# Constant key rows written as 32-bit words and shared by two engines, the plane join on GpSimd, one low part in six on ScalarE, and a new instruction order

## The chip, the cores and the metric

The kernel runs on one core of a Trainium2 chip. The metric is the device time of one execution in microseconds (us). The engines are TensorE (PE in the rows, its weight loads PEld), VectorE (DVE), ScalarE (ACT), GpSimd (POOL) and SyncE (SP), which issues every DMA of this kernel.

## The reference

Eight batches of eight attention heads (1152 keys of 64 values, queries averaged in pairs to 576 rows), then a channel mix over the joined heads.

```
q_pool = q.reshape(B, H, S // 2, 2, D).mean(axis=3)
scores = (q_pool @ k^T) / sqrt(D);  scores -= max(scores)
attn = exp(scores) / (sum(exp(scores)) + 1e-09);  a = attn @ v
x = a joined over heads            # 8 x 576 x 512
xk = mu_k * x + (1 - mu_k) * x_prev;  xr = mu_r * x + (1 - mu_r) * x_prev
out = sigmoid(xr @ w_r) * (relu(xk @ w_k) ** 2 @ w_v)
```

All inputs are fp32. The weights are 512x1024, 1024x512 and 512x512.

## The kernel before

The 64 heads run one after another. Each head has six blocks of 96 query rows, and a block has nine key chunks of 128. Operands are split into a high and a low half in fp16, so that products keep nearly fp32 accuracy.

**One block.** TensorE multiplies the keys (`ks1`) by the queries into a score buffer `s` in PSUM, of which there are three (L602). VectorE takes the maximum over the keys: in the first 14 heads (`n < N_ROW`) with L612, two small matmuls and a ScalarE instruction (L615 to L622), after that with L627 and four short steps that end at L648. The maximum goes into rows of the second query operand, and a second pass of matmuls with `ks2` (L653) adds the low halves and takes the maximum away. ScalarE writes the exponentials `pf` (L660). GpSimd writes their low part `pl` (L663) from the low 16 bits. TensorE multiplies both by the values (L741, L743 and L748 for whole windows of 128 rows, L712 for the half windows), in one PSUM bank `a`.

**The key buffers.** `ks2` has two buffers, for even and odd heads. Partitions 64 to 127 come by DMA from `ks1` (L551). Partitions 0 to 63 hold constants that never change: zeros, with one value in partition 0 and another in partition 1. They are written once, ahead of everything else, by three memsets on VectorE for each buffer (L448 to L450).

**Joining heads.** Two heads make a group `g` of four. For groups 4 to 30 of 32 (`CROSS`), `crossed` splits the fp32 result into two 16-bit planes (`xp`, L791), transposes them by DMA into `xd`, and joins the planes again into `xt` with three copies (L802): two of 64x128 elements and one of 128x1024. All of that runs on ScalarE before. The other five groups are turned by TensorE (L818).

**The channel mix.** When a batch of heads is finished, its rows go through two mixes (L953 to L964) and three products (L985), in tiles of 256 rows. This matmul work is spread between the blocks of the heads that follow. At the start the weights, which come as 64-bit floats, are decoded to fp16 pairs by ScalarE, VectorE and GpSimd (L856 to L874).

**The order.** Every operation is recorded by `op(engine, duration, function, ...)` with the buffers that it reads and writes. `Issue.run` then plays the list with the stated durations and chooses the order in which each engine issues its instructions. `MOVES`, `SEED` and `SPREAD` change priorities in that play at pseudo-random, each entry of `MOVES` in one stretch of time; three quarters of the entries fall within the first 170 us of the plan. The order is fixed in the program: an engine whose next instruction waits issues nothing behind it. What stands ahead of the recorded operations (constants, memsets) is issued first, in program order, on each engine.

Of the kernel before, what the change touches and what calls it, by code (L numbers as in the profile page):

```python
# [4 lines left out]

# [16 lines left out]
P = 128  # L22
# [17 lines left out]
CROSS = range(4, 31)  # L40
N_ROW = 14
PAIR = 99
GA = 0.045
XM = 3
SPLIT_ENG = 'ACT'
JOIN_ENG = 'ACT'
HALF_ENG = "ACT"
CROSS_LOAD, CROSS_MORE = 2.1, 0.5

# [38 lines left out]
WDEP = [("ks1", 1), ("ks2", 0), ("vr", 1)]  # L88
AHEAD2 = 0
MOVES, BASE, REACH = (  # L90
    34, 51, 119, 147, 174, 176, 191, 263, 328, 478, 600, 742, 785, 805, 941, 956, 1439, 1609, 3150, 4342,
    5377, 6334, 7410, 9224, 10224, 10571, 13731, 15873, 16751, 17268, 19136, 22188, 24107, 24376, 25583,
    25931, 31593,
), 2000000, 1150.0
SEED, SPREAD = 7, 1.0


class Issue:
# [224 lines left out]
def kernel(  # L323
# [63 lines left out]
    for a in range(P // U):  # L387
        part = slice(a * U, (a + 1) * U)
        nc.vector.memset(mask[part, a + 1:a + 2], 1.0 / SM)
        nc.gpsimd.tensor_copy(gather[part], ident[part, part].unsqueeze(1).broadcast_to([U, P // U, U]))  # L390
    nc.vector.memset(mask[0:U, 0:1], 1.0 / SM)

    kr, vr = bufs("kr", 2, [P, NC, D], F32), bufs("vr", 2, [P, NC, D], F32)
# [48 lines left out]
        nc.gpsimd.memset(t_[:, 1, :, 0:D], 0.0)  # L442
    for t_ in mx:
        nc.vector.memset(t_[:, 0:P - QN], 0.0)
    for t_ in md:
        nc.gpsimd.memset(t_, 0.0)
    for t_ in ks2:
        nc.vector.memset(t_[0:D], 0.0)  # L448
        nc.vector.memset(t_[0:2], -SM * 2.0 * EPS)
        nc.vector.memset(t_[0:1], -SM * (1.0 - EPS))  # L450
    for t_ in vt:
        nc.vector.memset(t_[:, :, 2 * D:2 * D + 2], 1.0)
    for t_ in vb:
# [128 lines left out]
    def block(n, j, i, t):  # L582

        hp, z = n % 2, i % 3
        qi = n // 2 % 2
        q0 = hp * TQ + j * QN
        qhi, qlo = (qT[qi][:, r].rearrange("p j x -> p (j x)")[:, q0:q0 + QN] for r in (0, 1))
        kh, kl = ([(t_, qi, c) for c in range(q0 // P, (q0 + QN - 1) // P + 1)] for t_ in ("qT", "qTl"))
        qm = [("qm", qi, q0)]
        s = s_b[z]  # L590
        p0 = (0 if hp else HW) + j * QN
        rows, us = slice(p0, p0 + QN), range(p0 // U, (p0 + QN) // U)

        def cols(c0, c1):
            return s[:, P + c0 * QN:P + c1 * QN]

        def grid(c0, c1):
            return cols(c0, c1).rearrange("p (c q) -> p c q", q=QN)

        def scores(c0, c1):  # L600
            for c in range(c0, c1):
                nc.tensor.matmul(cols(c, c + 1), ks1[hp][:, c, :], qhi,  # L602
                                 start=(c == c0), stop=False, skip_group_check=True)

        def first():
            for c0, c1 in BK:
                op("PE", (c1 - c0) * 0.0430, lambda c0=c0, c1=c1: scores(c0, c1),
                   r=[("ks1", hp), ("ks1", hp, 5)] + kh, w=[("s", z)], key=t)

        def row():  # L610
            mxz, mbz, y = mx[i % 2], mb[z], i % 2
            op("DVE", 0.975, lambda: nc.vector.tensor_reduce(mxz[:, P - QN:P], grid(0, NC).rearrange("p c q -> p q c"),  # L612
                                                             axis=AX.X, op=ALU.max),
               r=[("s", z)], w=[("mx", y)], key=t)
            op("PE", 0.059, lambda: nc.tensor.matmul(s[:, 0:P], mxz, identb, start=False, stop=False, skip_group_check=True),  # L615
               r=[("mx", y)], w=[("s", z)], key=t + O_MAX)
            op("DVE", 0.199, lambda: nc.vector.tensor_reduce(mbz, s[:, 0:P], axis=AX.X, op=ALU.max),
               r=[("s", z)], w=[("mb", z)], key=t + O_MAX)
            op("PE", 0.047, lambda: nc.tensor.matmul(s[:, 0:QN], mbz.broadcast_to([P, P]), negi[:, P - QN:P],
                                                     start=False, stop=False, skip_group_check=True),  # L620
               r=[("mb", z)], w=[("s", z)], key=t + O_MAX)
            op("ACT", 0.153, lambda: nc.scalar.activation(qlo[0:1], s[0:1, 0:QN], getattr(AF, ROW),  # L622
                                                          scale=(1.0 + EPS) / (1.0 - EPS), alpha=(1.0 - EPS) / (1.0 + EPS)),
               r=[("s", z)] + kl, w=qm, key=t + O_MAX)

        def top(y, a):
            op("DVE", 0.972, lambda: nc.vector.tensor_reduce(  # L627
                my[y][:, a], cols(0, NC).rearrange("p (x q) -> p x q", q=U), axis=AX.X, op=ALU.max, apply_transpose=True),
               r=[("s", z)], w=[("my", y)], key=t)

        def join(y, m):
            ql = qT[qi][0:U, 1].rearrange("p j x -> p (j x)")[:, q0 + QN - m * QN:q0 + QN]
            kls = kl if m == 1 else [("qTl", qi, c) for c in range((q0 - QN) // P, (q0 + QN - 1) // P + 1)]
            qms = [("qm", qi, q0 - x * QN) for x in range(m)]
            mr, got = s[:, 0:3 * m], s[0:U, U:U + 18 * m].rearrange("p (j k) -> p j k", k=6)
            mqz = mq[y][:, 0:3 * m]
            op("DVE", 0.062 + 0.028 * m, lambda: nc.vector.tensor_reduce(
                mr.rearrange("p (a j) -> p a j", j=3), my[y][:, 0:m].rearrange("p a (c j) -> p a j c", j=3), axis=AX.X, op=ALU.max),
               r=[("my", y)], w=[("s", z)], key=t + O_MAX)
            op("DVE", 0.061 + 0.019 * m, lambda: nc.vector.tensor_tensor(  # L640
                mqz, mr.unsqueeze(2).broadcast_to([P, 3 * m, 6]), mask.unsqueeze(1).broadcast_to([P, 3 * m, 6]), op=ALU.mult),
               r=[("s", z)], w=[("mq", y)], key=t + O_MAX)
            op("PE", GA, lambda: nc.tensor.matmul(s[:, U:U + 18 * m], gather.rearrange("p a x -> p (a x)"),
                                                  mqz.rearrange("p j k -> p (j k)"), start=False, stop=False, skip_group_check=True),
               r=[("mq", y)], w=[("s", z)], key=t + O_MAX)
            op("DVE", 0.055 + 0.031 * m, lambda: nc.vector.tensor_reduce(
                md[y][:, 0:3 * m, 0:2], windows(got, 5), axis=AX.X, op=ALU.max), r=[("s", z)], w=[("md", y)], key=t + O_MAX)
            op("DVE", 0.072 + 0.1 * m, lambda: nc.vector.transpose(ql, md[y][:, 0:3 * m].rearrange("p j x -> p (j x)")),  # L648
               r=[("md", y)] + kls, w=qms, key=t + O_MAX)

        def scores2(c0, c1):
            for c in range(c0, c1):
                nc.tensor.matmul(cols(c, c + 1), ks2[hp][:, c, :], qlo,  # L653
                                 start=False, stop=True, skip_group_check=True)

        def second():
            for c0, c1 in BK:
                op("PE", (c1 - c0) * 0.0430, lambda c0=c0, c1=c1: scores2(c0, c1),
                   r=[("ks2", hp)] + kl + qm, w=[("s", z)], key=t + O_EXP)
            op("ACT", NC * QN / 1200 + 0.06, lambda: nc.scalar.activation(  # L660
                pf[:, :, rows], grid(0, NC), AF.Exp, bias=SHIFT, scale=0.125 / (2.0 * SQ)),
               r=[("s", z)], w=[("pf", x) for x in us] + [("gate", i)], key=t + O_EXP)
            op("POOL", NC * QN / 1000 + 0.12, lambda: nc.gpsimd.tensor_scalar(  # L663
                pl[:, :, rows], half(pf, U16, 0)[:, :, rows], LO, 1.0, op0=ALU.mult, op1=ALU.mult),
               r=[("pf", x) for x in us], w=[("pl", x) for x in us], key=t + O_REST, port=True)

        return first, row, top, join, second

# [59 lines left out]
    def window(n, w, t):  # L728
# [37 lines left out]
        op("DVE", 0.08, lambda: nc.vector.reciprocal(dz, dz), r=[("den", z)], w=[("den", z)], key=t + O_EVAC)  # L766
        if n < X_ACT:
            for k_ in range(nk):
                op("ACT", 0.051 + D / 1200, lambda k_=k_: nc.scalar.activation(
                    xb[0][:, 2 * (k0 + k_) + hh], u[:, k_, 0:D], AF.Copy, scale=dz[:, k_:k_ + 1]),  # L770
                   r=[("den", z), ka], w=[("xb", 2 * (k0 + k_) + hh)], key=t + O_EVAC)
        else:
            op("DVE", 0.07 + nk * D / 960, lambda: nc.vector.tensor_tensor(  # L773
                xb[0][:, 2 * k0 + hh:2 * NW:2], u[:, :, 0:D], dz.unsqueeze(2).broadcast_to([P, nk, D]), op=ALU.mult),
               r=[("den", z), ka], w=[("xb", 2 * k_ + hh) for k_ in range(k0, NW)], key=t + O_EVAC)
# [2 lines left out]

    def copier(e, n):

        return {"POOL": (0.12 + n * 0.00113, nc.gpsimd.tensor_copy), "ACT": (0.093 + n / 1200, nc.scalar.copy),
                "DVE": (0.07 + n / 960, nc.vector.tensor_copy)}[e]

    def crossed(b, g, t):
# [268 lines left out]
        return key  # L1053


    queries(0, -20.0)
    prep(0, -20.0)
    prep(1, -10.0)
# [76 lines left out]
```

## Time and profile before

| | |
|---|---|
| median of 3 runs | 1095.19 us (1095.1 to 1096.24) |
| the profiled execution: its time | 1096.61 us |
| the profiled execution: its span | 1094.8 us |
| mean granted clock of TensorE | 0.995 |
| busy: PE, DVE, ACT, POOL | 1052.2, 920.7, 878.2, 593.6 us |
| read from HBM, written | 67.11 MB, 9.44 MB |

The span runs from the first to the last instruction, and 1.81 us of the execution's time lie outside it. Busy time of TensorE counts an instruction from its start to its modelled end, with overlaps counted once, so a high share does not say that its array is full. The granted clock is 1.0 for 2.4 GHz and 0.5 for 1.2 GHz; a value between them is a mean over a stretch.

### The profile page before, as it was taken

The page shows a single profiled execution, that of the slowest core. Times are in us where ns is not written, and L with a number is a line of the kernel's source. Part 1 is how long each engine was busy: PE and PEld are TensorE (multiplying, and loading weights), DVE is VectorE, ACT ScalarE, POOL GpSimd, SP SyncE. Part 2 cuts the span into 40 slices and gives each one's busy share as a digit, 9 for nine tenths or more (in the row PEclk, how much of TensorE's full clock was granted, in tenths as well). Part 3 has the DMA queues.
Part 4 walks back from the last instruction along what each step waited for, and adds up shares of the span by engine and source line. Part 5 has one row for each costly group of instructions (what it writes and reads, how often), then busy time and mean ns, then how long its engine had stood idle before and what let it go on. Part 6 is the DMA issues. An engine that isn't in the chain of part 4 may idle for free.

```text
span 1094.8 us, 43933 instructions
## 1 busy us (share of the span) xinstructions
PE 1052.2 (96%) x18521; PEld 858.5 (78%) x18521; DVE 920.7 (84%) x2400; ACT 878.2 (80%) x1604; POOL 593.6 (54%) x641
## 2 busy tenths in 40 slices
PE   5888899999999999999999999999999999999998
PEld 4777887978688887888787888878787978787565
DVE  8889888989899989998998998998889899975321
ACT  6999998978778888888887788887788887865643
POOL 3556685645555464654565465656465645554431
PEclk9999999999999999999999999999999999999999
DMA  8998955666666538674675655565656654510000
GB/s 204 234 233 201 192 131 130 140 142 111 134 124 121 123 71 179 128 132 79 143 157 100 143 125 124 122 141 113 134 113 130 143 116 89 90 40 12 20 28 22
DMA packets 254166, 134.52 MB, mean 123 GB/s; under 512 B 189456, under 2 KB 226320, under 8 KB 253968
## 3 DMA queue, kind: packets, MB, share of 16 engines
q1 hardware_dynamic: 253968, 131.71, 57.6%
q8 instruction: 145, 2.38, 0.9%
q14 instruction: 53, 0.43, 0.1%
HBM read 67.11 MB, written 9.44 MB: 70 GB/s over the span
## 4 chain that ended last, share of the span: by engine, by line
PE 82%; ACT 5%; DVE 5%; DMA 2%; issue 2%; POOL 0%; ACTq 0%; DVEq 0%
PE f L985 34%; PE s L602 11%; PE s L653 11%; PE a L748 5%; PE a L743 5%; PE a L741 5%; PE s L985 5%; ACT pf L660 2%; PE a L712 2%; PE a L985 2%; DMA ks<-kn 2%; DVE my L627 1%; ACT xt L802 1%; DVE mx L612 1%; DVE xm L956 1%
## 5 line engine op out<-in xcount | busy, mean ns | idle before, releaser
L663 POOL TENSOR_SCALAR pl<-pf 128x864 f16<-128x864 uint16 x384 | 384.3, 1001 | 360.0 <-ACT pf L660 322.4
L660 ACT ACTIVATE pf<-s 128x864 int32<-128x864 f32 x384 | 335.1, 887 | 89.2 <-PE s L653 40.2
L627 DVE TRANSPOSE_TENSOR_REDUCE my<-s 128x27 f32<-128x864 f32 x300 | 319.9, 1072 | 48.7 <-PE s L602 35.9
L602 PE MATMUL s<-qT,ks 128*128 128x96 f16 x3456 | 216.7, 207 | 11.7 <-ACT pf L660 10.6
L653 PE MATMUL s<-qT,ks 128*128 128x96 f16 x3456 | 211.5, 207 | 3.8 <-ACT qT L622 2.9
L602 PEld LDWEIGHTS <-ks 128*128 128x128 f16 x3456 | 181.5, 98 | 41.4 <-issue 16.0
L653 PEld LDWEIGHTS <-ks 128*128 128x128 f16 x3456 | 177.6, 98 | 26.8 <-issue 5.1
L743 PE MATMUL a<-vt,pf 128*128 128x64 f16 x2304 | 192.0, 194 | 0.4 <-issue 0.4
L741 PE MATMUL a<-vt,pf 128*128 128x65 f16 x2304 | 191.5, 193 | 0.4 <-DVE xb L773 0.4
L741 PEld LDWEIGHTS <-pf 128*128 128x128 f16 x2304 | 160.1, 99 | 4.6 <-issue 0.7
L743 PEld LDWEIGHTS <-pf 128*128 128x128 f16 x2304 | 154.7, 98 | 6.4 <-issue 1.2
L985 PE MATMUL f<-xhk,wk_hi 128*128 128x256 f16 x496 | 135.0, 272 | 0.0
L985 PE MATMUL f<-xlk,wk_hi 128*128 128x256 f16 x496 | 135.0, 272 | 0.0
L985 PE MATMUL f<-xhk,wk_lo 128*128 128x256 f16 x496 | 135.0, 272 | 0.0
L748 PE MATMUL a<-vb,pl 128*128 128x65 f16 x2304 | 122.8, 193 | 0.1
L985 PEld LDWEIGHTS <-wk_hi 128*128 128x128 f16 x1152 | 105.0, 98 | 11.5 <-issue 0.5
L1016 POOL TENSOR_TENSOR gl<-g 128x512 f16<-128x512 f32 x72 | 78.9, 1097 | 55.5 <-ACT g L1014 53.6
L748 PEld LDWEIGHTS <-pl 128*128 128x128 f16 x2304 | 97.3, 98 | 6.0 <-POOL pl L663 0.3
L612 DVE TENSOR_REDUCE mx<-s 128x96 f16<-128x864 f32 x84 | 87.3, 1052 | 16.3 <-PE s L602 5.6
L985 PE MATMUL f<-wv_hi,g 128*128 128x512 f16 x240 | 90.8, 378 | 2.1 <-ACT ex L1033 2.0
L985 PE MATMUL f<-wv_lo,g 128*128 128x512 f16 x240 | 90.9, 379 | 0.0
L985 PE MATMUL f<-wv_hi,gl 128*128 128x512 f16 x240 | 90.9, 379 | 0.0
(130 smaller groups left out, 2095.1 us busy)
## 6 DMA issues: line engine op xcount, KB each, us to landing
kr<-in_k_dram SPq DMA_DIRECT2D x64, 288.0 KB
vr<-in_v_dram SPq DMA_DIRECT2D x64, 288.0 KB
qr<-in_q_dram SPq DMA_DIRECT2D x63, 256.0 KB
ks<-ks SPq DMA_DIRECT2D x64, 144.0 KB
out_dram<-em SPq DMA_DIRECT2D x36, 256.0 KB
xt<-in_moe_w_k_dram SPq DMA_DIRECT2D x8, 512.0 KB
xt<-in_moe_w_v_dram SPq DMA_DIRECT2D x8, 512.0 KB
qr<-in_q_dram SPq DMA_DIRECT2D x32, 64.0 KB
```

Source lines behind the costliest of these rows:

```text
L602: nc.tensor.matmul(cols(c, c + 1), ks1[hp][:, c, :], qhi, start=(c == c0), stop=False, skip_group_check=True)
L612: op("DVE", 0.975, lambda: nc.vector.tensor_reduce(mxz[:, P - QN:P], grid(0, NC).rearrange("p c q -> p q c"), axis=AX.X, op=ALU.max), r=[( ...
L627: op("DVE", 0.972, lambda: nc.vector.tensor_reduce(my[y][:, a], cols(0, NC).rearrange("p (x q) -> p x q", q=U), axis=AX.X, op=ALU.max, app ...
L653: nc.tensor.matmul(cols(c, c + 1), ks2[hp][:, c, :], qlo, start=False, stop=True, skip_group_check=True)
L660: op("ACT", NC * QN / 1200 + 0.06, lambda: nc.scalar.activation(pf[:, :, rows], grid(0, NC), AF.Exp, bias=SHIFT, scale=0.125 / (2.0 * SQ)) ...
L663: op("POOL", NC * QN / 1000 + 0.12, lambda: nc.gpsimd.tensor_scalar(pl[:, :, rows], half(pf, U16, 0)[:, :, rows], LO, 1.0, op0=ALU.mult, o ...
L712: nc.tensor.matmul(a_b[z * HW:(z + 1) * HW, x0:x1], tb[:, c, p0:p0 + HW], vs[(n - 1 + z) % NV][:, c, r0:r0 + x1 - x0], skip_group_check=Tr ...
L741: nc.tensor.matmul(bank[:, a0:a0 + VN], half(pf, F16, 1)[:, c, rows], vt[jv][:, c, D:D + VN], start=(w == 1 and c == 0 and hh == 0), stop= ...
L743: nc.tensor.matmul(bank[:, a0:a0 + D], half(pf, F16, 1)[:, c, rows], vt[jv][:, c, 0:D], start=False, stop=False, skip_group_check=True)
L748: nc.tensor.matmul(bank[:, a0:a0 + VN], pl[:, c, rows], vb[jv][:, c, 0:VN], start=False, stop=(c == NC - 1), skip_group_check=True)
L985: nc.tensor.matmul(ps, terms[i][0], terms[i][1], start=(first and i == 0), stop=(i == last), skip_group_check=True)
L1016: op("POOL", 2 * n * 0.00203 + 0.08, lambda f2=f2: nc.gpsimd.tensor_tensor(gl[:, f2, 0:n], g32[:, f2, 0:n], gh[:, f2, 0:n], op=ALU.subtrac ...
```

## The change

1. The constant rows are written by a function `rows(engine, tile)`: zeros as before, and the two constant values as pairs of fp16 packed into one 32-bit word, so that a row is 576 words and not 1152 values. VectorE writes the first buffer ahead of everything. GpSimd writes the second, as a recorded operation.
2. The casts that fill `gather` and the memsets of `md` leave the prologue and become one recorded operation on GpSimd.
3. `JOIN_ENG` is `POOL`: the 128x1024 plane copy of L802 goes to GpSimd. The two 64x128 copies stay on ScalarE.
4. `PL_J = (5,)`: from head 14 on, the low part `pl` of the last of a head's six blocks is written by ScalarE.
5. The stated durations of some operations are altered, and `MOVES`, `SEED` with them, so the whole order is new.

```diff
-GA = 0.045
+GA = 0.03
+PL_J = (5,)
...
-JOIN_ENG = 'ACT'
+JOIN_ENG = 'POOL'
...
-    34, 51, 119, 147, 174, 176, 191, 263, 328, 478, 600, 742, 785, 805, 941, 956, 1439, 1609, 3150, 4342,
...
+    34, 54, 55, 67, 78, 129, 145, 371, 393, 692, 792, 1668, 1700, 2452, 3169, 3236, 3417, 3712, 4201, 4456,
...
-SEED, SPREAD = 7, 1.0
+SEED, SPREAD = 41, 1.0
...
-        nc.gpsimd.tensor_copy(gather[part], ident[part, part].unsqueeze(1).broadcast_to([U, P // U, U]))
...
-    for t_ in md:
-        nc.gpsimd.memset(t_, 0.0)
-    for t_ in ks2:
-        nc.vector.memset(t_[0:D], 0.0)
-        nc.vector.memset(t_[0:2], -SM * 2.0 * EPS)
-        nc.vector.memset(t_[0:1], -SM * (1.0 - EPS))
+    def rows(eng, t_):
+        eng.memset(t_[0:D], 0.0)
+        for r_, v_ in ((2, 2.0 * EPS), (1, 1.0 - EPS)):
+            two = struct.unpack("f", struct.pack("2e", -SM * v_, -SM * v_))[0]
+            eng.memset(t_[0:r_].rearrange("p c x -> p (c x)").bitcast(F32), two)
+
+    rows(nc.vector, ks2[0])
+
+    def later():
+        op("POOL", 2.2, lambda: rows(nc.gpsimd, ks2[1]), w=[("ks2", 1)], key=10.0)
+
+        def spread():
+            for a in range(P // U):
+                part = slice(a * U, (a + 1) * U)
+                nc.gpsimd.tensor_copy(gather[part], ident[part, part].unsqueeze(1).broadcast_to([U, P // U, U]))
+            for t_ in md:
+                nc.gpsimd.memset(t_, 0.0)
+
+        op("POOL", 1.7, spread, w=[("md", 0), ("md", 1), ("gather",)], key=60.0)
...
-            op("POOL", NC * QN / 1000 + 0.12, lambda: nc.gpsimd.tensor_scalar(
-                pl[:, :, rows], half(pf, U16, 0)[:, :, rows], LO, 1.0, op0=ALU.mult, op1=ALU.mult),
-               r=[("pf", x) for x in us], w=[("pl", x) for x in us], key=t + O_REST, port=True)
+            if n >= N_ROW and j in PL_J:
+                op("ACT", NC * QN / 1200 + 0.09, lambda: nc.scalar.activation(
+                    pl[:, :, rows], half(pf, U16, 0)[:, :, rows], AF.Copy, scale=LO),
+                   r=[("pf", x) for x in us], w=[("pl", x) for x in us], key=t + O_REST)
+            else:
+                op("POOL", NC * QN / 1000 + 0.127, lambda: nc.gpsimd.tensor_scalar(
+                    pl[:, :, rows], half(pf, U16, 0)[:, :, rows], LO, 1.0, op0=ALU.mult, op1=ALU.mult),
+                   r=[("pf", x) for x in us], w=[("pl", x) for x in us], key=t + O_REST, port=True)
...
-                op("ACT", 0.051 + D / 1200, lambda k_=k_: nc.scalar.activation(
+                op("ACT", 0.143 + D / 1200, lambda k_=k_: nc.scalar.activation(
...
+    later()
     queries(0, -20.0)
     prep(0, -20.0)
```

The other altered durations (the `DVE` steps of `top` and `join`, each by 0.006 to 0.010 us, and a plane copy if it ran on ScalarE) change what the order is made from, and no instruction.

## Rows read from the trace of the kernel before

**Rows 1.** The page: busy time by engine, and the chain's shares by engine.
```profile
PE 1052.2 (96%) x18521; PEld 858.5 (78%) x18521; DVE 920.7 (84%) x2400; ACT 878.2 (80%) x1604; POOL 593.6 (54%) x641
...
PE 82%; ACT 5%; DVE 5%; DMA 2%; issue 2%; POOL 0%; ACTq 0%; DVEq 0%
```
**Rows 2.** Busy time by stretch: window, length, engines, granted clock, DMA share, GB/s.
```profile
0.00:8.50 8.50, 0.00 (x0) 0.00 (x0) 6.19 (x24) 2.25 (x4) 3.91 (x16) 1.00 0.72 203
8.50:20.00 11.50, 9.29 (x149) 7.91 (x150) 10.59 (x24) 10.51 (x21) 2.69 (x3) 1.00 0.83 165
20.00:50.00 30.00, 23.18 (x487) 19.62 (x484) 27.50 (x50) 27.89 (x61) 15.68 (x18) 0.99 1.17 234
50.00:100.00 50.00, 43.18 (x948) 38.70 (x946) 43.20 (x76) 45.02 (x99) 30.44 (x32) 0.94 0.93 219
100.00:150.00 50.00, 44.95 (x888) 40.95 (x889) 43.61 (x75) 49.57 (x116) 35.66 (x37) 0.97 0.80 185
150.00:550.00 400.00, 393.47 (x7225) 324.05 (x7223) 363.52 (x959) 332.51 (x586) 225.28 (x237) 1.00 0.63 126
550.00:1000.00 450.00, 447.18 (x8253) 371.95 (x8252) 400.15 (x1155) 364.04 (x622) 251.72 (x268) 1.00 0.55 113
```
**Rows 3.** Instructions in order of time, 0 to 17 us: start, duration, what, idle before.
```profile
1.48 0.54 DVE L448 MEMSET ks<- 64x576 uint32 x1
...
2.31 1.02 DVE L449 MEMSET ks<- 2x1152 f16 x1 [0.29 <-DVE ks L448]
...
3.58 0.77 ACT L537 CAST kn<-kr 128x320 f16<-128x320 f32 x2 [1.36 <-DMA kr<-in_k_dram]
...
6.85 1.02 DVE L450 MEMSET ks<- 1x1152 f16 x1 [0.29 <-DVE ks L449]
...
7.98 0.47 DVE L540 TENSOR_TENSOR kn<-kr,kn 128x320 f16<-128x320 f32 x1
...
8.51 1.15 PE L515 MATMUL s<-identb,kn 128*128 128x128 f16 x9 [8.51 <-DVE kn L540]
...
16.93 2.16 POOL L663 TENSOR_SCALAR pl<-pf 128x864 f16<-128x864 uint16 x2 [12.02 <-ACT pf L660]
```
**Rows 4.** SP's own instructions in order of time, 0 to 60 us.
```profile
9.02 0.35 SPq L529 DMA_DIRECT2D kr<-in_k_dram  x1
...
18.95 0.50 SPq L551 DMA_DIRECT2D ks<-ks  x1
```
**Rows 5.** DMA rate in 40 equal slices of the first 12 us.
```profile
GB/s 0 0 0 0 0 31 154 238 306 361 310 133 147 248 62 254 386 327 333 328 342 272 273 304 329 229 180 162 139 56 10 1 0 123 154 338 307 92 215 200
```
**Rows 6.** Groups by line and shape: busy us, mean ns, idle before and releaser.
```profile
L537 ACT CAST kn<-kr 128x320 f16<-128x320 f32 x2 | 0.9, 460 | 1.4 <-DMA kr<-in_k_dram 1.4
...
L802 ACT COPY xt<-xd 128x1024 uint16<-128x1024 uint16 x27 | 36.7, 1359 | 1.3 <-DMA xd<-xp 1.2
L791 ACT COPY xp<-xb 128x1152 uint16<-128x1152 uint16 x27 | 31.2, 1155 | 2.7 <-DVE xb L773 2.6
...
L663 POOL TENSOR_SCALAR pl<-pf 128x864 f16<-128x864 uint16 x384 | 384.3, 1001 | 360.0 <-ACT pf L660 322.4 <-ACT qT L622 6.1 <-DVE qT L648 3.3
...
L442 POOL MEMSET qn<- 128x576 f16 x2 | 1.1, 577 | 0.1
...
L540 DVE TENSOR_TENSOR kn<-kr,kn 128x576 f16<-128x576 f32 x62 | 51.8, 836 | 0.0
```
**Rows 7.** TensorE's waits, 150 to 1050 us: total us, times, longest (first and last of seven).
```profile
PE s L602 <- ACT pf L660: 3.0, 6, 1.0
...
PE a L743 <- issue: 0.4, 1, 0.4
```
**Rows 8.** Busy time in the three stretches at half clock, columns as in group 2.
```profile
50.00:53.40 3.40, 3.40 (x59) 3.40 (x58) 2.38 (x3) 2.90 (x6) 1.68 (x2) 0.56 1.06 246
...
77.00:80.40 3.40, 3.19 (x36) 2.81 (x34) 2.47 (x6) 3.13 (x9) 2.38 (x2) 0.51 1.28 140
...
128.10:131.60 3.50, 3.28 (x40) 2.94 (x37) 2.77 (x6) 3.50 (x8) 1.82 (x2) 0.51 0.62 190
```

More of the change, by code (lines that the diff above doesn't have):

```diff
@@ L4 @@
 import random
+import struct
 import concourse.bass as bass
@@ L90 @@
 MOVES, BASE, REACH = (
-    34, 51, 119, 147, 174, 176, 191, 263, 328, 478, 600, 742, 785, 805, 941, 956, 1439, 1609, 3150, 4342,
-    5377, 6334, 7410, 9224, 10224, 10571, 13731, 15873, 16751, 17268, 19136, 22188, 24107, 24376, 25583,
-    25931, 31593,
[3 rows of a table added]
 ), 2000000, 1150.0
-SEED, SPREAD = 7, 1.0
+SEED, SPREAD = 41, 1.0
 class Issue:
@@ L626, in top @@
         def top(y, a):
-            op("DVE", 0.972, lambda: nc.vector.tensor_reduce(
+            op("DVE", 0.982, lambda: nc.vector.tensor_reduce(
                 my[y][:, a], cols(0, NC).rearrange("p (x q) -> p x q", q=U), axis=AX.X, op=ALU.max, apply_transpose=True),
@@ L636, in join @@
             mqz = mq[y][:, 0:3 * m]
-            op("DVE", 0.062 + 0.028 * m, lambda: nc.vector.tensor_reduce(
+            op("DVE", 0.07 + 0.028 * m, lambda: nc.vector.tensor_reduce(
                 mr.rearrange("p (a j) -> p a j", j=3), my[y][:, 0:m].rearrange("p a (c j) -> p a j c", j=3), axis=AX.X, op=ALU.max),
                r=[("my", y)], w=[("s", z)], key=t + O_MAX)
-            op("DVE", 0.061 + 0.019 * m, lambda: nc.vector.tensor_tensor(
+            op("DVE", 0.067 + 0.019 * m, lambda: nc.vector.tensor_tensor(
                 mqz, mr.unsqueeze(2).broadcast_to([P, 3 * m, 6]), mask.unsqueeze(1).broadcast_to([P, 3 * m, 6]), op=ALU.mult),
@@ L644, in join @@
                                                   mqz.rearrange("p j k -> p (j k)"), start=False, stop=False, skip_group_check=True),
-               r=[("mq", y)], w=[("s", z)], key=t + O_MAX)
-            op("DVE", 0.055 + 0.031 * m, lambda: nc.vector.tensor_reduce(
+               r=[("mq", y), ("gather",)], w=[("s", z)], key=t + O_MAX)
+            op("DVE", 0.063 + 0.031 * m, lambda: nc.vector.tensor_reduce(
                 md[y][:, 0:3 * m, 0:2], windows(got, 5), axis=AX.X, op=ALU.max), r=[("s", z)], w=[("md", y)], key=t + O_MAX)
-            op("DVE", 0.072 + 0.1 * m, lambda: nc.vector.transpose(ql, md[y][:, 0:3 * m].rearrange("p j x -> p (j x)")),
+            op("DVE", 0.08 + 0.1 * m, lambda: nc.vector.transpose(ql, md[y][:, 0:3 * m].rearrange("p j x -> p (j x)")),
                r=[("md", y)] + kls, w=qms, key=t + O_MAX)
@@ L779, in copier @@
     def copier(e, n):
-        return {"POOL": (0.12 + n * 0.00113, nc.gpsimd.tensor_copy), "ACT": (0.093 + n / 1200, nc.scalar.copy),
+        return {"POOL": (0.12 + n * 0.00113, nc.gpsimd.tensor_copy), "ACT": (0.093 + n / 1200 + (0.27 if n == 2 * (NW - 1) * P else 0.0), nc.scalar.copy),
                 "DVE": (0.07 + n / 960, nc.vector.tensor_copy)}[e]
```

2 rows, old and new, of the table AHEAD2 are left out of this document.

## The prediction

> **What bounds the kernel now.** I read the page first: TensorE is busy 96% of the span and holds 82% of the chain that ended last [rows 1]. So the question is where TensorE is not fed. The table by stretch answers it [rows 2]. From 150 to 1000 us TensorE is busy 840.65 of 850 us; it sets the pace, ScalarE works 696.6 of those 850 us, GpSimd 477.0. Up to 150 us it is idle for 8.5 + 2.2 + 6.8 + 6.8 + 5.1 = 29.4 us (each the length of a stretch less its PE figure), and there ScalarE is the full engine: 27.9 of 30, 45.0 of 50, 49.6 of 50 us. The largest single piece is the start: nothing runs on TensorE before 8.51 us.
>
> The timeline of the start shows why [rows 3]. The keys of head 0 have landed at 3.58 us and ScalarE casts them. The subtraction that makes their low halves (L540) stands on VectorE behind six memsets of `ks2`, three for each buffer, of which the first starts at 1.48 and the last at 6.85 us. It starts at 7.98, and the first matmul follows at 8.51. The row of the matmul names its releaser: DVE kn L540.
>
> **The rows in 32-bit words, on two engines.** A memset of 64x576 words took 0.54 us, one of 2x1152 fp16 values 1.02 [rows 3]: the price goes by elements, not by bytes or partitions. A constant row of 576 words I therefore price at 0.54, and an f32 memset of as many elements has no reason to differ from a uint32 one. VectorE now has three memsets in place of six. The first starts at 1.48 as before; each of the next two waits 0.29 us for the one ahead, as L449 and L450 do now: 1.48 + 3 x 0.54 + 2 x 0.29 = 3.68 us. The last one ends now at 6.85 + 1.02 = 7.87 and L540 starts 0.11 later, so VectorE could start it at 3.79. Then something else is last: ScalarE's cast of the first part, 3.58 + 0.46 [rows 6], 4.04 us, and about 0.06 us until VectorE sees it, which is my estimate from the 0.06 between L540's end at 8.45 and the matmul. So L540 starts at 4.1 and not at 7.98: **3.9 us earlier**. All steps behind it (transposes, copies, first scores, first exponentials) wait for one another and not for the DMAs, except where a later load has not landed.
>
> That exception I bound by the DMA row [rows 5]. Each slice is 0.3 us. The queue moves data from about 1.5 us, goes quiet at 9.0 to 9.6, and starts again with the keys that SP issues at 9.02, as soon as L540 has freed their buffer [rows 4]. So the first loads are all in by 9 us, at which time the earlier start needs nothing that today is used before 12.9. What was issued at 9.02 can be issued at 5.1, but its data queue behind the first loads. If the whole early part ran at the pace of the DMAs, only the quiet time could be won, about 0.9 us (three slices). From 20 to 50 us the DMA share is 1.17 [rows 2], so this can't be excluded. But TensorE's wait at the start names VectorE, and ScalarE, the full engine of the early part, is itself idle 8.5 - 2.25 us of the first 8.5. I take 3.9; the bounds are 0.9 and 3.9.
>
> **What GpSimd gets for it.** Three memsets of `ks2[1]`, at 0.58 each by its own 128x576 memset [rows 6]: 1.7 us. The casts to `gather` and the memsets of `md` are the same work, later. The cover is GpSimd's idle time: it waits 12.02 us before its first `pl` at 16.93 [rows 3]. The second `ks2` transfer, which needs its own buffer, is issued at 18.95 [rows 4]. Cost: nothing. Without that cover it would be the 1.7 us.
>
> **The join to GpSimd.** ScalarE loses 27 copies of 1.36, 36.7 us [rows 6]. GpSimd gains 27 copies of 1024 elements. Its nearest row is `pl`: 864 elements in 1.00 us, one input, 16 bits. In proportion that is 1.19 us, so 32 us in all. The lower bound is 27 us, if one took no longer than `pl`; the upper is twice 32, since a strided 16-bit write cost ScalarE as well: 1.36 us for 1024 elements here against 1.16 for 1152 in L791.
>
> **One low part in six to ScalarE.** Heads 14 to 63, one block each: 50 times. GpSimd loses 50 x 1.00 = 50 us. ScalarE reads every second 16-bit value as L791 does, 1152 elements in 1.16 us; in proportion 864 take 0.87 us, and by L802 (1.36 for 1024) 1.15. I take 0.9, the row nearest in kind: 45 us; the bounds are 43 and 57.
>
> Together ScalarE gets 45 - 36.7 = +8 us (6 to 20) and GpSimd 32 - 50 = -18 us (-23 to +14), spread over 180 to 1000 us, where ScalarE has some 150 us free and TensorE's waits are small: seven kinds, the largest 3.0 us in six times, for the exponentials that free a score buffer [rows 7]. No kind in that view waits for GpSimd. I put both moves at 0, with bounds of -3 (the 3.0 us of waits for ScalarE gone) and +6 (rival D).
>
> Here a rule of the skill speaks against the change. L540 over 128x576 takes 836 ns on average, and the two of 128x320 have their row at 0.47, so 0.84 is about what its length makes of it [rows 3, 6]; no row shown separates a delay in it. The Trainium skill (SBUF — State Buffer, "Who interferes with whom") says that a VectorE instruction with two SBUF inputs contends with a GpSimd instruction that reads SBUF, and whoever comes second is blocked for all of the other; one that only writes, as a memset, does not block it. By that rule the 27 joins each could hold VectorE for up to their 1.2 us, and 50 fewer `pl` give back more than that, so the sum would stay, with up to a microsecond of gain; the moved memsets would not hold L540 at the start. The sum does without it.
>
> **The new order.** It changes where the early 29.4 us and the three half-clock stretches lie. In those three TensorE was busy 3.40, 3.19 and 3.28 us at 1.2 GHz [rows 8]; at 2.4 GHz the same work would take half, so they cost up to 4.9 us. Each follows on a time in which TensorE had waited for others. Nothing in a trace tells what another order makes of this: the bounds are -4.9 (all three gone) and +4.9 (three more). Between equal ends I take the side on which an earlier start helps, -0.5, as ScalarE has 3.9 us more for the same early work.
>
> **The sum.** 1096.61 (the profiled execution) - 3.9 + 0 + 0 - 0.5 = 1092.2. That execution was 1.42 us above the median of the runs, so against the median: 1095.19 - 4.4 = **1090.8 us**. A measurement here tells 0.2%, 2.2 us, from no change: faster is below 1093.0, slower above 1097.4.
>
> **The rivals.**
> A, the forecast: the start's 3.9 us are kept to the end, 1089 to 1093. For it: from 150 us on TensorE is full, so work that comes earlier is not waited for again.
> B, the order also takes part of the early idle time: the 3.9, and the 4.9 us of half clock, 1095.2 - 8.8 = 1086.4. For it: 29.4 us of idle are there to be had. Against: ScalarE is 95% busy from 50 to 150 us, and nothing there takes work from it.
> C, the start is won and then lost: the early part goes at the pace of the DMAs, so 0.9 us remain, 1094.3, no change. For it: the DMA share of 1.17. Against: TensorE's early waits name VectorE and ScalarE.
> D, slower: the low part on ScalarE stands in front of the next head's exponentials or casts, and the three score buffers are not freed in time. It adds 0.9 us to that queue in 50 places. The time comes out slower if TensorE loses more than (3.9 + 2.2) / 50 = 0.12 us at each; with a third of each instruction lost, 0.3 x 50 = 15, less 3.9 and the 3.0 of today's waits, it would be 1103. Against: ScalarE is free 18% of that time, and loses the 1.36 us joins, which are longer and stand in the same queue.
> That the first part does nothing would need another reason for the start at 7.98, and the rows show none.
>
> **How the numbers follow.** A 0.50, B 0.20, C 0.17, D 0.13. Faster is A and B, 0.70; no change C, 0.17; slower D, 0.13. The predicted time is A's, 1090.8. For 8 in 10 the range goes down past B's 1086.4 to 1085.5, for an order that takes a little idle time as well, and up to 1097, over C's 1094.3 and the edge of D, which leaves out most of D and a little of B.
>
> **What would show it right or wrong.** The first matmul at about 4.6 us, with L540 at about 4.1 and three `ks2` memsets on VectorE. Idle time of TensorE up to 150 us near 25 us. L802's large copy on GpSimd at 1.2 us, 50 ScalarE rows with `pl` at 0.9. TensorE's waits from 150 to 1050 us still below 10 us. The prediction is wrong if the first matmul is early and the time at 150 us is not (C), if a new wait for ScalarE of some microseconds stands in TensorE's list (D), or if the granted clock up to 150 us has gone far from 0.94 to 1.0 either way (B, or its opposite).

## The result and the profile after

| | before | after |
|---|---|---|
| median | 1095.72 us (1095.1 to 1099.36) | 1084.37 us (1082.21 to 1085.36) |
| profiled execution: time, span | 1096.61, 1094.8 us | 1085.36, 1083.3 us |
| ratio | | 0.9887 (95% interval 0.986 to 0.9914) |

The kernel is 1.1% faster, 11.4 us by the medians of four runs each, where 4.4 were forecast, and the time lies 1.1 us under the range. From L452 on, the lines have moved by 15 to 20: L540 is now L555, L515 L530, L602 L617, L653 L668, L660 L675, L663 L683 (ScalarE's form L679), L802 L822, L985 L1005.

The page after, busy time by engine and the chain's shares, beside [rows 1]:

```profile
PE 1047.0 (97%) x18521; PEld 856.7 (79%) x18521; DVE 911.4 (84%) x2397; ACT 889.1 (82%) x1627; POOL 579.8 (54%) x621
...
PE 86%; ACT 4%; DVE 2%; issue 1%; DMA 1%; POOL 0%; SPq 0%; ACTq 0%; DVEq 0%
```

ScalarE has 10.9 us more to do and GpSimd 13.8 less. The table by stretch after, with the columns of [rows 2]:

```profile
0.00:8.50 8.50, 1.83 (x13) 1.25 (x14) 4.43 (x26) 3.86 (x8) 6.12 (x19) 1.00 0.77 206
8.50:20.00 11.50, 10.11 (x158) 8.87 (x158) 10.06 (x22) 9.62 (x21) 3.17 (x3) 1.00 0.82 205
20.00:50.00 30.00, 22.72 (x467) 20.03 (x463) 26.04 (x46) 26.49 (x59) 17.93 (x17) 0.94 1.17 236
50.00:100.00 50.00, 41.42 (x979) 37.67 (x977) 46.46 (x80) 47.50 (x107) 30.59 (x33) 1.00 0.96 215
100.00:150.00 50.00, 45.90 (x947) 41.72 (x946) 44.70 (x74) 49.64 (x112) 38.97 (x39) 1.00 0.74 188
150.00:550.00 400.00, 397.44 (x7329) 328.39 (x7327) 364.91 (x990) 340.84 (x606) 222.08 (x231) 1.00 0.61 128
550.00:1000.00 450.00, 448.25 (x8148) 370.24 (x8146) 392.85 (x1134) 370.27 (x637) 234.65 (x251) 1.00 0.55 111
```

TensorE is idle for 28.0 us up to 150 us (6.67 + 1.39 + 7.28 + 8.58 + 4.10); it was 29.4, and near 25 was forecast. From 150 to 1000 us it is busy 845.69 us and was 840.65, so its idle time there has fallen from 9.35 to 4.31 us. The early idle time, on which the forecast rested, has hardly changed, and the part of the run called full has become fuller. One stretch at half clock is left (35.5 to 38.9 us; the granted clock of 20 to 50 us is 0.94), where there were three [rows 8].

Busy time hides the clock and the shortest gaps, so I also worked out how much matmul work was done by a given time: every matmul of the trace counted with the usual distance to the next one of its shape at full clock (42 ns for 96 columns, 29 for 64 or 65, 109 for 256, 216 for 512). All kernels below have 1008.1 us of it.

```
work done by, us      20     50     100    150    350    550    1000
before                6.6   24.4   58.0   97.1  288.8  480.4  917.5
after                 7.3   24.5   59.5  101.3  296.2  489.7  929.0
after minus before    0.7    0.1    1.5    4.2    7.4    9.3   11.5
```

At 50 us nothing is won. 4.2 us are won by 150 us, and 7.3 more from there to 1000 us; 5.0 of those 7.3 are the idle time above. The start shows why so little is won by 20 us (instructions in order of time):

```profile
2.19 0.54 DVE L450 MEMSET ks<- 2x576 f32 x1 [0.17 <-DVE ks L447]
...
3.84 0.76 ACT L552 CAST kn<-kr 128x320 f16<-128x320 f32 x2 [1.62 <-DMA kr<-in_k_dram]
...
4.33 0.83 DVE L555 TENSOR_TENSOR kn<-kr,kn 128x320 f16<-128x320 f32 x2 [0.71 <-ACT kn L552]
...
4.88 1.14 PE L530 MATMUL s<-identb,kn 128*128 128x128 f16 x9 [4.88 <-DVE kn L555]
...
7.88 0.46 ACT L552 CAST kn<-kr 128x320 f16<-128x320 f32 x1 [1.41 <-DMA kr<-in_k_dram]
...
8.25 0.37 ACT L535 COPY qT<-a 128x256 f16<-128x256 f16 x1
...
8.66 1.60 PE L617 MATMUL s<-qT,ks 128*128 128x96 f16 x18 [1.93 <-ACT qT L535]
```

The subtraction starts at 4.33 us and was at 7.98 [rows 3]; the first matmul at 4.88, was 8.51. Then ScalarE stops at the cast of head 1's keys, which have not landed before 7.88 us, and the copy to `qT`, whose input TensorE had made by 6.35, stands behind it. The first scores come at 8.66. In the kernel before these keys were cast only at 9.85 us, with no wait, and the first scores came at 10.63:

```profile
9.85 0.46 ACT L537 CAST kn<-kr 128x320 f16<-128x320 f32 x1
...
10.63 1.57 PE L602 MATMUL s<-qT,ks 128*128 128x96 f16 x18 [0.55 <-ACT qT L520]
```

The rest of the lead goes between 34 and 39 us. There TensorE waits 1.9 us for queries that a transposing DMA brings (the one wait of this kind up to 150 us), and then runs 3.4 us at half clock (0.50):

```profile
PE s L617 <- DMA qT<-qn: 1.9, 1, 1.9
...
35.50:38.90 3.40, 2.97 (x44) 3.00 (x45) 1.06 (x1) 1.36 (x2) 0.95 (x2) 0.50 1.26 215
```

Groups by line and shape after, beside [rows 6]:

```profile
L683 POOL TENSOR_SCALAR pl<-pf 128x864 f16<-128x864 uint16 x334 | 331.9, 994 | 333.9 <-ACT pf L675 285.6 <-PE a L768 12.4 <-DVE mq L655 7.9
...
L555 DVE TENSOR_TENSOR kn<-kr,kn 128x576 f16<-128x576 f32 x62 | 53.7, 866 | 0.2 <-issue 0.2
L679 ACT ACTIVATE pl<-pf 128x864 f16<-128x864 uint16 x50 | 46.4, 927 | 0.3
...
L822 POOL COPY xt<-xd 128x1024 uint16<-128x1024 uint16 x27 | 37.7, 1395 | 15.4 <-DMA xd<-xp 14.6
```

A join costs GpSimd 1.40 us and ScalarE cost 1.36; GpSimd waits 14.6 us for the transfers ahead of it. TensorE's waits from 150 to 1050 us, first and last group, beside [rows 7]:

```profile
PE s L617 <- ACT pf L675: 1.7, 4, 0.6
...
PE f L1005 <- POOL xlk L984: 0.3, 1, 0.3
```

### The profile page after: what moved, and what is told of

It reads as the page before. It is cut to its first block, busy times and chain, and to the rows that moved or that the text cites. A ratio compares the mean times of both kernels' runs of the same rounds, so it can differ in the third digit from the quotient of the medians.

```text
span 1083.3 us, 43992 instructions
## 1 busy us (share of the span) xinstructions
PE 1047.0 (97%) x18521; PEld 856.7 (79%) x18521; DVE 911.4 (84%) x2397; ACT 889.1 (82%) x1627; POOL 579.8 (54%) x621
## 4 chain that ended last, share of the span: by engine, by line
PE 86%; ACT 4%; DVE 2%; issue 1%; DMA 1%; POOL 0%; SPq 0%; ACTq 0%; DVEq 0%
PE f L1005 36%; PE s L668 12%; PE s L617 12%; PE a L763 6%; PE a L768 6%; PE a L761 6%; PE s L1005 5%; PE a L732 2%; PE a L1005 2%; ACT pf L675 2%; DVE my L642 1%; DVE mx L627 0%; PE s L658 0%; ACT xb L789 0%; DVE kn L555 0%
## 5 line engine op out<-in xcount | busy, mean ns | idle before, releaser
L683 POOL TENSOR_SCALAR pl<-pf 128x864 f16<-128x864 uint16 x334 | 331.9, 994 | 333.9 <-ACT pf L675 285.6
L675 ACT ACTIVATE pf<-s 128x864 int32<-128x864 f32 x384 | 336.0, 887 | 79.1 <-PE s L668 46.5
L617 PE MATMUL s<-qT,ks 128*128 128x96 f16 x3456 | 215.9, 207 | 14.9 <-ACT pf L675 10.3
L668 PE MATMUL s<-qT,ks 128*128 128x96 f16 x3456 | 213.2, 206 | 2.7 <-ACT qT L637 2.0
L617 PEld LDWEIGHTS <-ks 128*128 128x128 f16 x3456 | 180.8, 98 | 40.1 <-issue 18.9
L668 PEld LDWEIGHTS <-ks 128*128 128x128 f16 x3456 | 177.9, 98 | 26.9 <-issue 4.1
L1005 PE MATMUL f<-xlk,wk_hi 128*128 128x256 f16 x496 | 135.0, 272 | 0.3 <-POOL xlk L984 0.3
L1005 PE MATMUL f<-xhk,wk_hi 128*128 128x256 f16 x496 | 135.1, 272 | 0.2
L1005 PE MATMUL f<-xhk,wk_lo 128*128 128x256 f16 x496 | 135.1, 272 | 0.0
L1005 PEld LDWEIGHTS <-wk_hi 128*128 128x128 f16 x1152 | 105.6, 98 | 10.8 <-issue 0.4
L1005 PE MATMUL f<-wv_lo,g 128*128 128x512 f16 x240 | 90.9, 379 | 0.0
L1005 PE MATMUL f<-wv_hi,gl 128*128 128x512 f16 x240 | 90.8, 379 | 0.0
L1005 PE MATMUL f<-wv_hi,g 128*128 128x512 f16 x240 | 90.8, 378 | 0.0
```

The lines of the kernel that those rows point to most:

```text
L617: nc.tensor.matmul(cols(c, c + 1), ks1[hp][:, c, :], qhi, start=(c == c0), stop=False, skip_group_check=True)
L668: nc.tensor.matmul(cols(c, c + 1), ks2[hp][:, c, :], qlo, start=False, stop=True, skip_group_check=True)
L683: op("POOL", NC * QN / 1000 + 0.127, lambda: nc.gpsimd.tensor_scalar(pl[:, :, rows], half(pf, U16, 0)[:, :, rows], LO, 1.0, op0=ALU.mult, ...
L1005: nc.tensor.matmul(ps, terms[i][0], terms[i][1], start=(first and i == 0), stop=(i == last), skip_group_check=True)
```

## The experiments

Three parts had to be told apart: the rows at the start, the moves between engines, and the order. Ratios are to the kernel before on the same chip, with their 95% intervals; 0.1% is 1.1 us.

**The rows alone, with each order kept.** The order of recorded work stays exactly that of the kernel edited.

```diff
 e1, in the kernel before (gather and md go behind these on GpSimd)
-    for t_ in ks2:
-        nc.vector.memset(t_[0:D], 0.0)
...
+    rows(nc.vector, ks2[0]), rows(nc.gpsimd, ks2[1])
 e3, in the changed kernel: the six memsets on VectorE again, and
-        op("POOL", 2.2, lambda: rows(nc.gpsimd, ks2[1]), w=[("ks2", 1)], key=10.0)
+        op("POOL", 2.2, lambda: None, w=[("ks2", 1)], key=10.0)
```

> The kernel before with only the new constant rows (32-bit words, second buffer on GpSimd, gather and md behind it); the order of every engine is that of before. Theory P (the start is kept, as forecast): first matmul near 4.9 us and the end 3.9 us earlier, ratio 0.9964. Theory O (the gain of the whole change is the new order): first matmul near 4.9 us, but the first scores wait for something later and no more than 1 to 2 us are left at the end, ratio 0.998 to 1.0. Theory E (the gain is the work moved between ScalarE and GpSimd) says the same as O here.

> The changed kernel with the old memsets (six on VectorE, first matmul near 8.5 us again); the order of all recorded work is the new one. Theory P: loses 3.9 us of the 11.3, ratio to before 0.993. Theory O: loses 0 to 2 us, ratio 0.989 to 0.9905. Theory E: as O.

Measured: e1 1094.85 us, 0.9984 (0.9971 to 0.9998). e3 1087.82 us, 0.9922 (0.9905 to 0.994), against 0.9887 with the rows. TensorE's first matmul and first scores in e1 (instructions in order of time):

```profile
4.84 1.14 PE L515 MATMUL s<-identb,kn 128*128 128x128 f16 x9 [4.84 <-POOL ks L448]
...
8.40 1.60 PE L602 MATMUL s<-qT,ks 128*128 128x96 f16 x18 [1.99 <-ACT qT L520]
```

The matmul's row names a memset of GpSimd, which ended a part in the same moment; the weight load of the same matmuls names DVE kn L540. In the old order too 3.7 us are won at the first matmul and 2.2 at the first scores (10.63 before), and 1.8 us are left at the end by the ratio (0.2 to 3.2), as theory O had it. In the new order the rows are worth 3.8 by the ratios, nearer to theory P, but the two intervals overlap a little. So the rows are worth some 2 to 4 us, not sharply measured: half of what the first matmul wins in one order, about all of it in the other.

**An earlier start of the scores.** In the changed kernel, the cast and the subtraction of head 1's keys and one sum of queries are put behind the copies to `qT`.

```diff
+        late = [at("ACT", ("kn", 1, 0)), at("DVE", ("qs", 2)), at("DVE", ("knl", 1, 0))]
+        order = [n for n in order if n not in late]
+        x = 1 + max(order.index(at(*k)) for k in (("ACT", ("qT", 0, 0)), ("DVE", ("qTl", 0, 0))))
+        order[x:x] = late
```

> The changed kernel with three instructions of the start put behind the copies of the first queries: the cast and the subtraction of head 1's keys and one sum of queries, which wait for transfers, now stand behind the copies to qT on ScalarE and VectorE; TensorE's, GpSimd's and SyncE's orders are unchanged. First scores near 7.0 us in place of 8.66. Theory P (a start that is earlier stays earlier): 1.5 us faster than the changed kernel, ratio to before near 0.9875. Theory C (the early part is paced by something else): no change against the changed kernel, 0.988 to 0.990.

Measured: 1085.72 us, 0.9894 (0.9876 to 0.9913), no change. Its instructions in order of time:

```profile
6.66 1.60 PE L639 MATMUL s<-qT,ks 128*128 128x96 f16 x18
8.43 0.76 ACT L574 CAST kn<-kr 128x256 f16<-128x256 f32 x2 [1.82 <-DMA kr<-in_k_dram]
9.67 0.50 PE L552 MATMUL a<-identb,qn 128*128 128x128 f16 x3 [1.41 <-ACT qn L526]
9.90 0.68 ACT L593 ACTIVATE vt<-vr 128x576 f16<-128x576 f32 x1 [0.29 <-DMA vr<-in_v_dram]
```

The scores come 2.0 us earlier, and then ScalarE waits for the keys and the values of the next loads. By 30 us TensorE has started 335 matmuls (339 in the changed kernel): nothing is left of the 2.0 us. The busy time from 30 to 40 us, in e12 and then in the changed kernel, whose wait and half clock fall there:

```profile
30.00:40.00 10.00, 8.69 (x222) 7.91 (x220) 9.37 (x16) 9.76 (x19) 7.79 (x8) 1.00 1.14 237
...
30.00:40.00 10.00, 7.56 (x173) 7.21 (x171) 6.27 (x12) 6.94 (x14) 5.32 (x6) 0.83 1.25 225
```

So the lead that e12 shows at 50 us by my count (27.1 us of work, 24.5 in the changed kernel) comes from those 10 us and not straight from the scores. At 100 us it is 60.1 against 59.5. Two stretches at half clock fall between 80 and 104 us in this run, which the changed kernel does not have there. What else eats the lead was not separated. Theory C's time came true, theory P's did not.

**The engines alone, with each order kept.** e2 puts the new engines at the old places, e4 the old engines at the new places, e5 only the joins.

```diff
 e2, in the kernel before: pl of block 5 from head 14 on by nc.scalar.activation, and
-            d, f = copier(e, 2 * n_)
+            d, f = copier(e, 2 * n_)[0], nc.gpsimd.tensor_copy if y == 2 else copier(e, 2 * n_)[1]
 e4 and e5, in the changed kernel (e4 also: all pl by nc.gpsimd.tensor_scalar)
-            d, f = copier(e, 2 * n_)
+            d, f = copier(e, 2 * n_)[0], nc.scalar.copy if y == 2 else copier(e, 2 * n_)[1]
```

> The kernel before with only the two moves between engines (large plane copy to GpSimd, the low part of the last block from head 14 on to ScalarE), each at its old place in the order; the start is that of before. Theory E: the 6.5 us that the changed kernel gains between 150 and 650 us appear, ratio 0.994. Theory O: within 0.2% of before, or slower, since the order was not made for these engines. Theory P: no change.

> The changed kernel with the large plane copies back on ScalarE and all low parts on GpSimd, each at its place in the new order. Theory E: the 6.5 us between 150 and 650 us are lost, ratio to before 0.995. Theory O: loses less than 2 us, ratio 0.989 to 0.991.

> The changed kernel with only the large plane copy back on ScalarE, each copy at its place in the new order; the low parts stay where the change put them. Theory J (putting both moves back cost 16 us because 27 copies of 1.36 us, placed for an engine that may wait, now stand in ScalarE's queue in front of exponentials): loses 13 to 18 us against the changed kernel, ratio to before 1.00 to 1.006. Theory L (it was the low parts going back to GpSimd): loses at most 2 us, ratio 0.989 to 0.991.

Measured: e2 1097.39 us, 1.0009 (0.9998 to 1.002). e4 1100.29 us, 1.0039 (1.0024 to 1.0054). e5 1097.77 us, 1.0016 (1.0 to 1.0031). In the old order the new engines win nothing (theory O). In the new order the old engines lose 16.7 us by the ratio, which neither theory for e4 had; 14 of them are lost by the joins alone (theory J). TensorE's waits from 150 to 1050 us in e4 have grown most here:

```profile
PE s L617 <- ACT pf L675: 7.8, 12, 0.9
PE s L668 <- DVE qT L663: 2.5, 5, 0.9
```

At 150 us e4 has done 102.6 us of work, more than the changed kernel; at 1000 us 914.3 against 929.0. So an order is made for its engines: 27 copies of 1.36 us on ScalarE, at places chosen for GpSimd, cost the kernel 0.5 us each (14.1 / 27). This is not the price of the move. That needs an order planned for each.

**The order: nudges, durations, seed.** With an empty list of nudges the order is what the planner finds by itself.

```diff
-MOVES, BASE, REACH = (
-    34, 54, 55, 67, ...
+MOVES, BASE, REACH = (
 ), 2000000, 1150.0
```

e6 is this in the kernel before, e7 in the changed one, e8 in the changed one with `JOIN_ENG = 'ACT'` and `PL_J = ()`. e9 is e6 with the new stated durations, e10 e6 with seed 41, e11 e7 with seed 7.

> The kernel before with an empty list of nudges (MOVES), so its order is the planner's own. Theory S (the list is worth most of what the new order gains): at least 8 us slower than before, ratio 1.007 or more. Theory R (the engines and durations, not the list, make the order better): within 3 us of before, ratio 0.997 to 1.003.

> The changed kernel with an empty list of nudges. Theory S: loses all but the start's gain, so it lies near the kernel before with an empty list less 2 to 4 us. Theory R: loses at most 3 us of its 11, ratio to before 0.989 to 0.992.

> The changed kernel with an empty list of nudges, the plane copies on ScalarE and all low parts on GpSimd, planned anew with these engines. Theory E2 (with the copies on GpSimd the planner finds a better order by itself): 5 to 8 us slower than the changed kernel with an empty list. Theory S: within 2 us of it.

> The kernel before with an empty list of nudges and the new stated durations (ScalarE's copies dearer, GA smaller, VectorE's short steps a little dearer); all instructions, engines and rows are those of before. Theory D (stated durations nearer to the measured ones give a better order): 3 to 5 us faster than the kernel before with an empty list, ratio to before 0.995 to 0.997. Theory N (of the 6 us between that kernel and the changed one with old engines and no list, all is the rows and the seed): within 1.5 us of before, ratio 0.9985 to 1.0015.

> The kernel before with an empty list of nudges and the new seed (41), nothing else. It shows how far one start of the planner is from another. Theory D: within 1.5 us of before. Theory Z (the seed found a better order): 3 us faster or more, ratio 0.997 or less.

> The changed kernel with an empty list of nudges and the old seed (7). Theory D and the engines: ratio to before 0.989 to 0.992, as with the new seed. Theory Z: 3 us or more slower than with the new seed, ratio 0.993 or more.

| | median, us | ratio |
|---|---|---|
| e6, before, no list | 1095.36 | 0.9996 (0.9984 to 1.0008) |
| e7, after, no list | 1085.07 | 0.9898 (0.9878 to 0.9919) |
| e8, as e7 with old engines | 1089.38 | 0.9943 (0.9923 to 0.9964) |
| e9, e6 with new durations | 1096.31 | 0.9995 (0.9983 to 1.0007) |
| e10, e6 with seed 41 | 1094.78 | 0.9982 (0.997 to 0.9993) |
| e11, e7 with seed 7 | 1092.6 | 0.9962 (0.9948 to 0.9976) |

The lists do nothing that can be measured, in either kernel; theory S fell. The durations do nothing (theory N). The seed does (theory Z): the changed kernel with the old seed has a third of the gain. By the ratios the other seed costs the new kernel 7.0 us (e7, e11) and is worth 1.5 to the old (e6, e10, with intervals that overlap), so e8's loss of 4.3 us, 4.9 by the ratio, could be the engines or luck. That was left to pairs under other seeds.

> The changed kernel with an empty list of nudges, seed 7, plane copies on ScalarE and all low parts on GpSimd, planned for these engines. Its pair with the new engines took 1092.6 us. Theory E2 (the moves between engines are worth some 4 us once the order is planned for them): near 1096, ratio 1.0. Theory Z (only the seed counts, and the pair at seed 41 differed by chance): within 2 us of its pair, 1090.5 to 1094.5, or faster than it.

> The changed kernel with an empty list and seed 1. Theory Z: seeds differ by several us; a seed that nobody chose gives 1087 to 1095, and the chosen 41 stays among the best. Theory E2 alone, with no luck in the seed: near 1085, as with seed 41.

> As the run before it with the old engines, planned for them, seed 1. Theory E2: 3 to 6 us slower than its pair. Theory Z: a difference of either sign.

> The changed kernel with an empty list and seed 2. Theory Z: 1087 to 1095. Theory E2 with no luck in the seed: near 1085.

> As the run before it with the old engines, planned for them, seed 2. Theory E2: 3 to 6 us slower than its pair. Theory Z: a difference of either sign.

> The changed kernel with an empty list and seed 3. Theory Z: 1087 to 1095, slower than seed 41. Theory E2 with no luck in the seed: near 1085.

| seed | new engines | old engines | difference |
|---|---|---|---|
| 41 | 0.9898 | 0.9943 | -0.45% |
| 7 | 0.9962 | 1.0005 (0.9993 to 1.0017) | -0.43% |
| 1 | 0.9974 (0.9961 to 0.9987) | 0.9968 (0.9957 to 0.998) | +0.06% |
| 2 | 0.9994 (0.9982 to 1.0006) | 0.9984 (0.9969 to 0.9999) | +0.10% |
| 3 | 0.9971 (0.9956 to 0.9985) | | |

Over the four seeds other than 41, the changed kernel without a list has a mean ratio of 0.9975, 2.7 us faster than before, between 0.7 and 4.2. Seed 41 lies 8.4 us below that mean (0.9975 - 0.9898 = 0.77%). The engines are worth 4.9 and 4.7 us under two seeds; under the other two they lose 0.7 and 1.1, less than the intervals can tell from nothing. The mean is 2 us, and four pairs don't settle its sign: e13 came as theory E2 had it, e15 and e17 did not. Seed 2 with the new engines (1096.37 us) lies above the times that theory Z gave. Seed 41 is good with the old engines too (0.9943, where the other three have 0.9968 to 1.0005). How it was found is not on record; as the best of five it is in part a lucky draw.

The table by stretch, 0 to 150 and 150 to 1000 us, of e7 (seed 41):

```profile
0.00:150.00 150.00, 121.17 (x2555) 108.42 (x2556) 132.49 (x245) 137.96 (x305) 98.94 (x111) 1.00 0.90 209
150.00:1000.00 850.00, 846.17 (x15473) 698.99 (x15472) 758.27 (x2123) 711.45 (x1241) 457.48 (x480) 1.00 0.57 119
```

and of e11 (seed 7):

```profile
0.00:150.00 150.00, 122.05 (x2502) 109.03 (x2503) 131.02 (x243) 137.20 (x303) 97.58 (x109) 0.99 0.97 211
150.00:1000.00 850.00, 841.83 (x15476) 696.63 (x15475) 762.52 (x2116) 707.88 (x1227) 464.24 (x479) 1.00 0.58 118
```

By my count e7 has done 102.1 us of work at 150 us and the other four 100.0, 96.7, 100.1 and 97.5; from 150 to 1000 us e7 does 827.3 us and they 819.1 to 823.8. The chosen seed is ahead in both parts. From 150 us on TensorE is idle 3.8 us under it and 7.5 in the mean under the others. Which of its placements makes it so, no run shows.

A part of the difference is the clock. Over 130 executions of the kernel before, on five chips, the time falls by 0.64 us for each 0.001 that the mean granted clock is higher. That clock was 0.9945 in them and 0.999 in the four executions of the changed kernel; it was 0.9994 in e7 and 0.9973 in the mean of the other four seeds. By that, as an estimate, fewer stretches at half clock give 2.9 of the 11.4 us, and 1.4 of seed 41's 8.4.

## Why the prediction was wrong

**The rows: the first steps right, the way to the end not.** L540 was forecast at 4.1 us and starts at 4.33, since the first keys land 0.26 us later than in the profile before. An f32 memset of 576 took 538 ns, as taken; the waits between them were 0.17, not 0.29. GpSimd's three took 1.05 + 0.57 + 0.57 us, 2.2 and not 1.7, in time in which it had nothing else. The exception that the forecast allowed, a later load that has not landed, is what came. It compared the end of the first loads, 9 us, with a use at 12.9, but head 1's keys were used at 9.85; 3.9 us earlier is 5.95, and they land just before 7.88. (The quiet time in its DMA row runs to 9.9 us, three slices as it counted, not to 9.6.) So the first scores come 2.0 us earlier and not 3.9: rival C's mechanism, for a part. At 50 us the changed kernel has no lead, yet 1.8 us of the rows' gain reach the end in e1 and 3.8 in e3. The forecast of 3.9 lies at the upper edge of that.

**The joins and low parts: sizes right, price open.** ScalarE's `pl` took 927 ns (0.9 taken), GpSimd's join 1.40 us (1.19 taken, within the bounds), ScalarE's net load rose by 46.4 - 36.7 = 9.7 us (8). The price of 0 stands within what the pairs give, -4.9 to +1.1, but its bound of -3 may be too narrow: I took it from TensorE's listed waits for ScalarE, and in e4, which lost 16.7 us, the largest of them grew by 6.1 (1.7 to 7.8). Rival D did not come: TensorE's waits from 150 us on fell.

**The order: the step that failed.** I priced it at -0.5 and bounded it by 4.9 us either way, from the three half-clock stretches alone. It is worth some 8 us against other seeds of the same kernel, and about 60% of that (5.8 of 9.3 us, against the mean of the four by the count of work) is won after 150 us, in a part that I had called full because TensorE was busy 840.65 of 850 us. The 9.35 us of idle that this leaves were more than the whole forecast gain, and I gave the new order nothing of them; 5.0 were won. The other 2.3 of the 7.3 us won there don't show in busy time: TensorE does 820.4 us of work, by the count, in those 850 us before and 827.7 after. Rival B had the sign and nearly the time (1086.4), but that is luck for the most part: it placed 8.8 us before 150 us, where only 4.2 of the 11.5 are won, and its half-clock term of 4.9 is 2.9 by the estimate above.

**VectorE's subtraction beside GpSimd.** The forecast read L540's mean of 836 ns as what its length makes of it, and saw no delay. The rows of single instructions show one: 747 ns in the median, and up to 1606 before and 1736 after. The longest after, the copy of a join that ran ahead of it, and the line's shortest, median and longest time:

```profile
817.31 1.36 POOL L822 COPY xt<-xd 128x1024 uint16<-128x1024 uint16 x1 [1.76 <-DMA xd<-xp]
817.48 1.74 DVE L555 TENSOR_TENSOR kn<-kr,kn 128x576 f16<-128x576 f32 x1
...
L555 DVE TENSOR_TENSOR kn<-kr,kn x66: 416/741/1736, 4.3 to 935.6; 128x576 f16<-128x576 f32 x62, 128x320 f16<-128x320 f32 x2, 128x256 f16<-128x256 f32 x2
```

The subtraction ends 0.55 us after the copy. In the changed kernel 14 of the 62 whole subtractions took more than 0.8 us; each of them began while a GpSimd instruction ran and ended 0.55 to 0.62 us after it, and 15 of 62 did so before. This agrees with the Trainium skill (SBUF — State Buffer, "Who interferes with whom"): the second to come waits for all of the first. Only two of the 62 met a join in this way, far from 27, since most of them found GpSimd idle or came first. In e5, the same order with the joins on ScalarE, the group is:

```profile
L555 DVE TENSOR_TENSOR kn<-kr,kn 128x576 f16<-128x576 f32 x62 | 51.2, 825 | 0.0
```

That is 2.5 us less over all 62 than the 53.7 with the joins on GpSimd. Of the gain that the forecast drew from the rule this group shows nothing: it took 51.8 us before [rows 6]. The sums of queries (L501), which read two inputs as well, took 855 ns with the joins on GpSimd and 860 without. No run separates what of this reaches the end.

## What to carry to other kernels

When a change brings a new schedule, price the schedule as a term of its own, and take its size from other seeds of the same planner: here five seeds of one kernel lay up to 10 us apart, and all other parts of the change were worth 0.7 to 4.2 us under the four that were not chosen. A busy share of 99% is not full: of the 9.35 us that it left, 5.0 were won. Test a move between engines with an order planned for it, and under several seeds; in an order made for the other engine it costs something else (16.7 us here, nothing clear of the interval the other way round). A start that is earlier is worth only what the next transfer lets through, so look for what lands last behind it.

## What was not expected of the hardware

GpSimd's memset of 64x1152 fp16 zeros stayed 1152 elements long and took 1.05 us, while VectorE's of the same line ran as 576 words in 0.54:

```profile
1.47 0.54 DVE L447 MEMSET ks<- 64x576 uint32 x1
...
3.11 1.05 POOL L447 MEMSET ks<- 64x1152 f16 x1
```

GpSimd copied 1024 16-bit values in 1.40 us, where its `pl` takes 0.99 for 864: 18% more for each value (1.36 against 1.15 ns).
